# Attention, mixture layer and gated layer on one core: forms of y and the gate-times-value product move from GpSimd to VectorE, and the scheduler gets new urgencies and costs

## The chip, the cores and the metric

The kernel runs on one core of a Trainium2 chip. TensorE (PE) multiplies matrices, VectorE (DVE), ScalarE (ACT) and GpSimd (POOL) work elementwise, SyncE (SP) issues the transfers (DMA). The metric is the device time of one execution in microseconds; a kernel's time is the median of its runs.

## The reference

```
a   = softmax(causal(q @ k.T / 8)) @ v                 # 4 batches, 8 heads, 576 tokens, 64 wide
mem = (phi(q) @ M_prev) / (phi(q) @ z_prev + 1e-6)     # phi(x) = elu(x) + 1
x   = g * mem + (1 - g) * a                            # g = sigmoid(beta); x is 2304 x 512
r   = relu(x @ w_in)                                   # 512 -> 2048
x2  = (s * r * r + b) @ w_out                          # 2048 -> 512
out = (sigmoid(x2 @ w_gate) * (x2 @ w_val)) @ w_out2   # 512 -> 1536 -> 512
```

All of it is float32.

## The kernel before

**Arithmetic.** Each float32 operand of a large product is split into a high part, rounded by ACT, and a low part, the rest, subtracted by DVE (for some of them by POOL). TensorE adds three products of parts.

**Attention (the first third).** There are 16 jobs: job j is one batch and one pair of heads. Jobs 0 to 3, batch 0, take a path of their own (called direct, lines 1000 to 1380). For each job PE transposes k and q (`kt`, `qt`), ACT and DVE split them into `KT` and `QT`, PE makes scores (`sc`, L1139 and L1163 on the direct path, L712 and L738 on the other), DVE masks them and takes the largest of each row into the tile `P` (L692), ACT takes the exponential (`P`, L1179 or L754), PE transposes `P` (`pt`, L1232 or L843, in groups A to D), ACT and DVE copy or split these into `PT_A`, `PT_B`, and PE multiplies them with v (`o`, L1272, or `acc`, L896 on). PE also multiplies phi(q) with the memory (`ret`, L1084). The direct path's results are scaled by DVE into `X` (L1290) and transposed by PE (`xt`, L1306) into x.

**h.** When all of a batch's x is there, PE computes h = x @ w_in (L330, 1536 matmuls in all). This needs no other work beside it and is spread between the later jobs' attention work. Before its use w_in is loaded (`raw_w_in`) and split (`f_w_in` on ACT at L261, then L264 to L273 on DVE). ACT applies relu and r goes to a scratch tensor in DRAM.

**y.** y is summed over 96 steps: 6 windows of 384 tokens, 16 steps each. A step loads r (`rr`), ACT squares it and rounds it to `gh`, DVE subtracts `gl` (L1525), and PE does 12 matmuls (L1540), the last four with `gl`. `gh` and `gl` have rings of four buffers each. Beside this runs the preparation of the gate and value weights in 12 blocks of `raw_gv` (split), `wm` (sums of blocks, DVE L1654), `wp` (high and low parts, ACT L1669 and DVE L1672), stored to a scratch tensor.

**The gated layer.** Windows are taken in three pairs; a pair's gate and value products use a scheme with 7 products in place of 8. It needs sums and differences of quarters of y, the forms: `yf`, `yg` by subtraction (`less`, L1726) and `yt` by splitting (high by ACT at L1717, low at L1721). A pair has 11 such elementwise operations on 128 x 768 elements, of which five are POOL's and six DVE's. Then for 12 groups a pair, six of gate and six of value, PE makes seven products `m` (L1808, 6 matmuls each); DVE adds them up in `set` (L1820), ACT applies the sigmoid, POOL multiplies gate and value into `p` (L1830, 72 operations of 128 x 384 in all), ACT and DVE split `p` into `ps` (L1882, L1895) and PE multiplies with w_out2 (`o`, L1905). The split of w_out2 runs beside the first pair.

**What sets the order.** Nothing of the order is written out by hand. A planner, the class `Plan`, gets each piece of work with its engine, its estimated duration, an urgency and its inputs; it plays the program through with these durations, always starts the ready task with the lowest urgency, and the instructions are emitted in the order found. `late` is how long after its end a task's result reaches another engine. The urgencies come from the table `TUNE`. On the chip every engine takes its own instructions in the order emitted and waits where an input isn't there.

Of the kernel before, what the change touches and what calls it, by code (L numbers as in the profile page):

```python
# [43 lines left out]
class Plan:  # L44
# [6 lines left out]
    def add(self, eng, ns, fn, urgency, reads=(), writes=(), new=(), late=60, size=0, port=0):  # L51

# [104 lines left out]
def attention_moe_kernel(  # L157
# [18 lines left out]
    P = 128  # L176
# [201 lines left out]
    def keys(t):  # L378
        return min((t + 1) * P, S)
# [109 lines left out]
    def mm(n):  # L489
        return max(57, 5 + 0.4375 * n)  # L490
# [4 lines left out]
    def act(n):  # L495
        return 150 + 0.86 * n

    def act2(n):
        return 190 + 0.85 * n

    def dve(n):
        return 152 + 1.05 * n

    def dve2(n):
        return 150 + 1.05 * n
# [43 lines left out]
    def plan_prep(j):  # L549
# [91 lines left out]
        def f_hi():  # L641
# [13 lines left out]
        add("DVE", 1200, phi_s, w, reads=[("phit", j), ("gates", 0)], new=[("nrm", ("nrm", j))])  # L655
# [5 lines left out]
            "ACT", 2 * act(n), f_hi, w, reads=[("ft", j)],  # L661
# [3 lines left out]
            "DVE", 2 * dve(n), lambda: stack_lo(T.pop(("ft", j)), T["FS", j]), w,  # L665
# [32 lines left out]
    def plan_scores(j):  # L698
# [79 lines left out]
        for m, ts in enumerate(groups):  # L778
            w = u + m * AT["tile"]
            if ts[0] < NT4:  # L780
                add(
                    "PE", sum(3 * mm(keys(t)) for t in ts) + 60, lambda ts=ts: score(ts), w,
# [11 lines left out]
            for part in range(2):  # L794
                for t in ts:
                    if part and t == NT4:
# [4 lines left out]
                        "DVE", dve(n) + 90, fn, w + part, reads=[("sc", j, part, ts[0]), ("sums", j)],  # L801
# [4 lines left out]
                        "ACT", 290 + 0.85 * n + 190, lambda e=part, t=t: exps(e, t), w + part,  # L806
                        writes=[("P", j, part, t), sums[part][-1]], reads=[("sums", j)],
                    )
        for part in range(2):
# [3 lines left out]
                "DVE", 450, lambda part=part, cols=cols: rsums(part, cols), w + part,  # L813
# [22 lines left out]
    def plan_products(j):  # L836
# [94 lines left out]
        for m, g in enumerate(gs):  # L931
# [3 lines left out]
            if g not in ("B1", "B2", "D0", "D1"):  # L935
                new.append((tag, ("PT", j, g)))
            key = ("PT", j, "B0" if tag == "PTB" else g)
# [1113 lines left out]
```

## Time and profile before

| | us |
|---|---|
| median of 3 runs | 1063.08 |
| lowest, highest | 1060.46, 1063.38 |
| profiled execution, its time | 1061.53 |
| its span on the chip | 1059.7 |
| PE busy | 1039.0 |
| DVE busy | 693.0 |
| ACT busy | 565.6 |
| POOL busy | 316.9 |

The span runs from the first to the last instruction on the core. The mean granted clock of TensorE was 0.994 of full speed. An engine counts as busy only while it executes: waiting for a semaphore is not in it.

### The profile page before, as it was taken

How to read it: one execution, taken by the hardware profiler on the slowest of the kernel's cores; microseconds unless marked ns; L12 is line 12 of the kernel's file. 1: busy time of each engine (PE TensorE's matmuls, PEld its weight loads, DVE VectorE, ACT ScalarE, POOL GpSimd, SP SyncE). 2: the span in 40 equal slices, each digit the busy share in tenths (PEclk: the TensorE clock that was granted, in tenths of full speed). 3: DMA queues.
4: the chain of work that ended last, by engine and by line, in shares of the span. 5: the costliest groups of instructions: out<-in, count | busy, mean ns of one | idle time of the engine just before them, and what ended most of it. 6: DMA issues, size and time to landing. Idle time of an engine off the chain costs nothing.

```text
span 1059.7 us, 18856 instructions
## 1 busy us (share of the span) xinstructions
PE 1039.0 (98%) x6696; PEld 980.9 (93%) x6696; DVE 693.0 (65%) x1414; ACT 565.6 (53%) x1223; POOL 316.9 (30%) x373
## 2 busy tenths in 40 slices
PE   6999999999999999999999999999999999999998
PEld 4888999999999999999999999998899998899986
DVE  5788887766676637669888765778525576155531
ACT  6587877777777647566867663335212243111230
POOL 2346565544444402310400002445102252033200
PEclk9899999999999999999999999999999999999999
DMA  5544443333222138659699977992368730677400
GB/s 135 132 110 121 132 133 114 102 86 89 77 71 67 51 128 306 212 175 356 220 306 362 381 269 268 325 320 88 116 218 253 254 103 30 206 249 257 153 25 35
DMA packets 159694, 186.46 MB, mean 176 GB/s; under 512 B 70256, under 2 KB 135280, under 8 KB 159600
## 3 DMA queue, kind: packets, MB, share of 16 engines
q1 hardware_dynamic: 158384, 184.96, 53.8%
q8 instruction: 53, 0.87, 0.3%
q10 hardware_dynamic: 1216, 0.30, 0.1%
q14 instruction: 41, 0.34, 0.1%
HBM read 138.03 MB, written 47.19 MB: 175 GB/s over the span
## 4 chain that ended last, share of the span: by engine, by line
PE 94%; ACT 2%; DMA 1%; DVE 1%; issue 1%; SPq 0%; POOL 0%; POOLq 0%; DVEq 0%
PE m L1808 25%; PE h L330 19%; PE y L1540 18%; PE o L1905 14%; PE sc L712 3%; PE acc L896 2%; PE o L1272 2%; PE acc L897 2%; PE pt_B L843 1%; PE acc L900 1%; PE sc L738 1%; PE kt L459 1%; PE pt_A L843 1%; PE pt_D L843 1%; DMA raw_w_in<-in_moe_w_in_dram 1%; PE qt L459 1%
## 5 line engine op out<-in xcount | busy, mean ns | idle before, releaser
L1808 PE MATMUL m<-yt,ws 128*128 128x384 f32 x1512 | 262.8, 334 | 0.0
L1808 PEld LDWEIGHTS m<-yt,ws 128*128 128x128 f32 x1512 | 262.2, 188 | 0.3
L330 PE MATMUL h<-x,w_in 128*128 128x256 f32 (+1 forms) x1536 | 223.9, 300 | 1.0 <-ACT r L340 1.0
L330 PEld LDWEIGHTS h<-x,w_in 128*128 128x128 f32 x1536 | 209.2, 190 | 3.7 <-ACT r L340 1.9
L1820 DVE TENSOR_TENSOR set<-m,set 128x384 f32<-128x384 f32 x252 | 135.7, 555 | 99.3 <-PE m L1808 91.4
L1905 PE MATMUL o<-w_out,ps 128*128 128x512 f32 x648 | 152.1, 396 | 0.6 <-DVE ps L1895 0.6
L1540 PE MATMUL y<-gh,w_out 128*128 128x384 f32 (+1 forms) x768 | 150.8, 338 | 0.7 <-ACT r L340 0.5
L1905 PEld LDWEIGHTS o<-w_out,ps 128*128 128x128 f32 x648 | 121.7, 188 | 29.9 <-DVE ps L1895 1.0
L1540 PEld LDWEIGHTS y<-gh,w_out 128*128 128x128 f32 x768 | 135.4, 188 | 1.4 <-ACT r L340 0.8
L1830 POOL TENSOR_TENSOR p<-set,set 128x384 f32<-128x384 f32 x72 | 75.8, 1057 | 187.7 <-DVE set L1820 187.0
L282 POOL TENSOR_TENSOR w_out<-raw_w_out,w_out 128x512 fp32r<-128x512 f32 x28 | 37.6, 1342 | 215.9 <-DVE set L1820 127.8
L340 ACT ACTIVATE r<-h 128x320 f32<-128x320 f32 (+1 forms) x128 | 51.8, 411 | 67.1 <-PE h L330 59.6
L692 DVE CUSTOM_DVE_ANT_0 P<-sc,mask 128x256 f32<-128x256 f32 (+4 forms) x144 | 68.7, 517 | 23.7 <-PE sc L712 17.4
L1540 PE MATMUL y<-gl,w_out 128*128 128x384 f32 x384 | 82.9, 337 | 0.0
L1816 ACT COPY set<-m 128x384 f32<-128x384 f32 x36 | 17.3, 480 | 111.1 <-PE m L1808 111.1
L770 POOL TENSOR_SCALAR P<-P,rs 128x384 f32<-128x384 f32 (+4 forms) x108 | 65.7, 630 | 25.8 <-DVE rs L766 25.0
L1525 DVE TENSOR_TENSOR gl<-rr,gh 128x384 fp32r<-128x384 f32 x96 | 58.0, 613 | 22.1 <-PE y L1540 15.6
L1895 DVE TENSOR_TENSOR ps<-p,ps 128x512 fp32r<-128x512 f32 x54 | 46.2, 883 | 35.7 <-ACT ps L1882 35.5
L1540 PEld LDWEIGHTS y<-gl,w_out 128*128 128x128 f32 x384 | 68.6, 188 | 0.0
L1824 ACT ACTIVATE set<-set 128x384 f32<-128x384 f32 x72 | 37.6, 524 | 57.1 <-DVE set L1820 57.1
L754 ACT ACTIVATE P<-P,nm 128x384 f32<-128x384 f32 (+4 forms) x108 | 62.5, 581 | 9.4 <-DVE nm L692 9.0
L1882 ACT CAST ps<-p 128x512 fp32r<-128x512 f32 x54 | 32.0, 620 | 65.8 <-PE o L1905 51.8
(185 smaller groups left out, 1504.2 us busy)
## 6 DMA issues: line engine op xcount, KB each, us to landing
ws<-weight_scratch SPq DMA_DIRECT2D x108, 512.0 KB, 4.6
rr<-relu_scratch SPq DMA_DIRECT2D x96, 192.0 KB, 5.6
weight_scratch<-wp SPq DMA_DIRECT2D x36, 512.0 KB, 6.6
raw_w_out<-in_moe_w_out_dram SPq DMA_DIRECT2D x28, 512.0 KB, 6.0
relu_scratch<-r SPq DMA_DIRECT2D x32, 320.0 KB, 2.7
ws<-weight_scratch SPq DMA_DIRECT2D x36, 256.0 KB, 3.1
raw_w_in<-in_moe_w_in_dram SPq DMA_DIRECT2D x16, 512.0 KB, 4.2
relu_scratch<-r SPq DMA_DIRECT2D x32, 256.0 KB, 2.3
```

Of the source, the lines that this page charges most:

```text
L330: nc.tensor.matmul(t[:, :n], wt[:, wi, c], x[:, xi, c], start=(m == 0), stop=(m == 3 * NK - 1))
L340: nc.scalar.activation(rts[b, c0, f - f % 2][:, f % 2, :n], t[:, :n], AF.Relu)
L692: nc.vector.tensor_tensor_reduce(out=pr, in0=ps, in1=mk, scale=1.0, scalar=3e38, op0=ALU.add, op1=ALU.min, accum_out=nm,)
L754: nc.scalar.activation(pr, pr, AF.Exp, bias=T.pop(("nm", j, e, t)), scale=-1.0, accum_out=T["sums", j][:, col : col + 1],)
L770: nc.gpsimd.tensor_scalar(out=pr, in0=pr, scalar1=T["rs", j, part][:, n : n + 1], scalar2=1.0, op0=ALU.mult, op1=ALU.mult,)
L1525: nc.vector.tensor_tensor(out=gl, in0=r_sb.pop(step)[:, :n], in1=gs[step][0][:, :n].bitcast(F32), op=ALU.subtract,)
L1540: nc.tensor.matmul(accs[wi][d][:, : y.shape[1]], w_out_sb[f][:, x, d], y, start=(f == 0 and x == 0 and y is gh), stop=(f == NF - 1 and y i ...
L1808: nc.tensor.matmul(acc, wt[:, a, k : k + P], yt[:, y, c], start=(m == 0), stop=(m == 3 * K2 - 1),)
L1820: nc.vector.tensor_tensor(out=t[:, o], in0=Z["m", z, x], in1=t[:, i], op=ALU.add)
L1830: engine[TIMES[o]].tensor_tensor(out=p[:, f + HF * OF[o][0], OF[o][1]], in0=Z["set", z][:, o], in1=Z["set", zg][:, o], op=ALU.mult,)
L1895: nc.vector.tensor_tensor(out=part(t, 1, i), in0=src(i), in1=part(t, 0, i).bitcast(F32), op=ALU.subtract,)
L1905: nc.tensor.matmul(Z["zo", z], Z["ps", z, i][:, a, k * P : (k + 1) * P], w_out2_sb[f][:, x].rearrange("p c f -> p (c f)"), start=(i == k = ...
```

## The change

- The two groups of forms named above go to DVE: all 11 operations of a pair are now DVE's, 15 more than before in three pairs.
- `TIMES`, the engine of the four products gate x value of a gate group and its value group, is DVE for all: 72 operations.
- P's transposes by PE are a task that in the planner now waits until the target tile `PT` is free. The wait is one of the planner: on the chip the transposes write PSUM and only the copy out of it touches `PT`; what changes is where the transposes stand in PE's order. A matching `p_copy` allocates the tile for whichever group comes first.
- The planner's durations of ACT and DVE work are lower, its `late` for both is higher, and those of PE's score tasks rise by 200 ns.
- All urgencies of `TUNE` are new numbers.

PE's and ACT's instructions are the same ones in another order; DVE has 87 more instructions and POOL 87 fewer.

```diff
 TUNE = {
-    "mem": -190592.6, "lq": 1410.0, "lk": -51988.3, "lv": 48155.5, "lm": 1334.3,
+    "mem": -167048.5, "lq": 2645.2, "lk": -2618.3, "lv": 75766.9, "lm": 2921.8, "q": -48985.8,
...
-    def add(self, eng, ns, fn, urgency, reads=(), writes=(), new=(), late=60, size=0, port=0):
+    def add(self, eng, ns, fn, urgency, reads=(), writes=(), new=(), late=None, size=0, port=0):
+        if late is None:
+            late = {"ACT": 160, "DVE": 145}.get(eng, 60)
...
     def act(n):
-        return 150 + 0.86 * n
+        return 50 + 0.86 * n
...
     def dve(n):
-        return 152 + 1.05 * n
+        return 68 + 1.05 * n
...
-                    "PE", sum(3 * mm(keys(t)) for t in ts) + 60, lambda ts=ts: score(ts), w,
+                    "PE", sum(3 * mm(keys(t)) for t in ts) + 260, lambda ts=ts: score(ts), w,
...
+                if g in ("A0", "B0"):
+                    add("BAR", 0, lambda: None, w, new=[(f"PT{g[0]}", ("PT", j, g))], late=0)
                 add(
                     "PE", flip(nb), lambda g=g: trans(g), w,
-                    reads=sorted({("P", j, e, t) for e, t, k0 in UNITS[g]}),
-                    new=[("s" if nb <= 4 else "w", ("pt", j, g))]
-                    + ([(f"PT{g[0]}", ("PT", j, g))] if g in ("A0", "B0") else []), late=250,
+                    reads=sorted({("P", j, e, t) for e, t, k0 in UNITS[g]}) + [("PT", j, WINS[win][0])],
+                    new=[("s" if nb <= 4 else "w", ("pt", j, g))],
+                    late=250,
                 )
...
-        add("ACT", 675, scaled, u, reads=[("raw", key)], new=[(fl, ("f", key))])
-        add("DVE", **port(1120), fn=rest, urgency=u, writes=[("raw", key)])
+        add("ACT", 573, scaled, u, reads=[("raw", key)], new=[(fl, ("f", key))])
+        add("DVE", **port(950), fn=rest, urgency=u, writes=[("raw", key)])
...
-        plan_split(B21, "B21", "POOL")
+        plan_split(B21, "B21", "DVE")
         plan_split(B22, "B22", "DVE")
-        plan_less("B11", "B12", "B11", "POOL")
+        plan_less("B11", "B12", "B11", "DVE")
         plan_split(T1, "B11", "DVE")
-        plan_less("B12", "B22", "B12", "POOL")
+        plan_less("B12", "B22", "B12", "DVE")
         plan_less("B22", "B22", "B11", "DVE")
-        plan_split(T2, "B22", "POOL")
+        plan_split(T2, "B22", "DVE")
         plan_split(T3, "B12", "DVE")
-        plan_less("B21", "B21", "B22", "POOL")
+        plan_less("B21", "B21", "B22", "DVE")
...
-    TIMES = ("POOL", "POOL", "POOL", "POOL")
+    TIMES = ("DVE", "DVE", "DVE", "DVE")
```

Three places in the new order matter below. In the listings a row is a line, an operation, output and inputs, and the shape.

PE early in the program, behind job 0's first scores; before:

```order
L1084 MATMUL ret_1_206<-mem_144,phi_169 128x65
L1090 MATMUL ret_0_205<-mem_144,phi_169 64x65 x2
L1163 MATMUL sc_4_237<-KT_147,QT_160 128x288 x6
L1232 MATMUL pt_A_262<-ident,P_0_0_230 128x128
L1232 MATMUL pt_A_262<-ident,P_0_1_244 128x128 x2
L1232 MATMUL pt_A_279<-ident,P_1_0_250 128x128
L1232 MATMUL pt_A_279<-ident,P_1_1_258 128x128 x2
L1139 MATMUL sc_0_2_291<-KT_147,QT_160 128x384
```

The same place of the changed kernel:

```order
L1143 MATMUL sc_1_2_205<-KT_151,QT_161 128x384
L1167 MATMUL sc_4_217<-KT_151,QT_161 128x288 x6
L1143 MATMUL sc_0_3_252<-KT_151,QT_161 128x512
L1143 MATMUL sc_1_3_253<-KT_151,QT_161 128x512
L1143 MATMUL sc_0_3_252<-KT_151,QT_161 128x512
L1143 MATMUL sc_1_3_253<-KT_151,QT_161 128x512
L1143 MATMUL sc_0_3_252<-KT_151,QT_161 128x512
L1143 MATMUL sc_1_3_253<-KT_151,QT_161 128x512
L1236 MATMUL pt_A_277<-ident,P_0_0_228 128x128
L1236 MATMUL pt_A_277<-ident,P_0_1_233 128x128 x2
```

All scores of job 0 now stand ahead of the transposes of its first `P` and of `ret`, which stood between them. In the same way all of job 1's scores now stand ahead of job 0's first `o`; SP loads the first `raw_w_in` and job 1's q ahead of `mem`, which they followed; ACT has the first `f_w_in` ahead of job 0's first exponential, and it stood behind the copy of `PT_A`.

DVE in the y stage at the first steps of the third window (`gl_2` on), where the forms of the first pair become possible; before:

```order
L1525 TENSOR_TENSOR gl_1_7175<-rr_1_7005,gh_1_7152 128x384
L1525 TENSOR_TENSOR gl_2_7181<-rr_2_7031,gh_2_7173 128x384
L1584 TENSOR_SCALAR yf_7179<-y_1_6761,sb_s,sb_c 128x384
L1584 TENSOR_SCALAR yf_7179<-y_3_6763,sb_s,sb_c 128x384
L1525 TENSOR_TENSOR gl_3_7207<-rr_3_7042,gh_3_7203 128x384
L1721 TENSOR_TENSOR yt_0_7205<-yf_6757,yt_0_7205 128x768
L1525 TENSOR_TENSOR gl_4_7232<-rr_4_7081,gh_4_7228 128x384
```

and of the changed kernel, from behind `gl_1` of that window:

```order
L1677 TENSOR_TENSOR wp_1_7156<-wm_7110,wp_1_7156 128x512
L1677 TENSOR_TENSOR wp_2_7162<-wm_7110,wp_2_7162 128x512
L1677 TENSOR_TENSOR wp_3_7167<-raw_gv_1_6922,wp_3_7167 128x256
L265 TENSOR_SCALAR raw_gv_0_7016<-raw_gv_0_7016 128x512
L268 SCALAR_TENSOR_TENSOR raw_gv_0_7016<-raw_gv_0_7016 128x512
L1589 TENSOR_SCALAR yf_7190<-y_1_6765,sb_s,sb_c 128x384
L1589 TENSOR_SCALAR yf_7190<-y_3_6767,sb_s,sb_c 128x384
L274 SCALAR_TENSOR_TENSOR raw_gv_0_7016<-f_gv_0_7170,raw_gv_0_7016 128x512
L1726 TENSOR_TENSOR yt_0_7214<-yf_6780,yt_0_7214 128x768
L1726 TENSOR_TENSOR yt_1_7216<-yf_6780,yt_1_7216 128x768
L1731 TENSOR_TENSOR yf_6780<-yf_7190,yf_6780 128x768
L1726 TENSOR_TENSOR yt_6_7219<-yf_7190,yt_6_7219 128x768
```

Before, the window's second and third `gl` stand next to each other; now twelve operations, weight blocks and forms, stand between them.

DVE at the end of the first pair's products, ahead of the first `ps` that follow the last group; before:

```order
L1820 TENSOR_TENSOR set_11_9649<-m_11_4_9696,set_11_9649 128x384
L1721 TENSOR_TENSOR yt_5_9704<-yf_8360,yt_5_9704 128x768
L1820 TENSOR_TENSOR set_11_9649<-m_11_6_9708,set_11_9649 128x384
L1721 TENSOR_TENSOR yt_6_9731<-yf_8732,yt_6_9731 128x768
L1895 TENSOR_TENSOR ps_0_2_9736<-p_8898,ps_0_2_9736 128x512
```

and of the changed kernel:

```order
L1825 TENSOR_TENSOR set_11_9645<-m_11_4_9697,set_11_9645 128x384
L1835 TENSOR_TENSOR p_8927<-set_11_9645,set_5_9554 128x384 x3
L1825 TENSOR_TENSOR set_11_9645<-m_11_6_9709,set_11_9645 128x384
L1835 TENSOR_TENSOR p_8927<-set_11_9645,set_5_9554 128x384
L1900 TENSOR_TENSOR ps_0_2_9736<-p_8927,ps_0_2_9736 128x512
```

The forms of the next pair that stood there have moved away, and the four products `p` of the last group stand in DVE's row instead of POOL's.

## Rows read from the trace of the kernel before

**Rows 1.** The page's span in 40 equal slices of 26.5 us, tenths.

```profile
PE   6999999999999999999999999999999999999998
...
PEclk9899999999999999999999999999999999999999
```

**Rows 2.** The page's chain of work that ended last, by engine.

```profile
PE 94%; ACT 2%; DMA 1%; DVE 1%; issue 1%; SPq 0%; POOL 0%; POOLq 0%; DVEq 0%
```

**Rows 3.** Busy time in stretches of the span; columns in the first row.

```profile
core 0: us, PE busy (x) PEld busy (x) DVE busy (x) ACT busy (x) POOL busy (x), PEclk, DMA share, GB/s
0.00:20.00 20.00, 12.02 (x81) 9.52 (x82) 9.30 (x34) 9.81 (x20) 6.08 (x34) 0.91 0.65 152
20.00:40.00 20.00, 17.60 (x138) 15.79 (x137) 13.95 (x38) 12.48 (x25) 4.01 (x4) 0.83 0.55 125
...
620.00:642.00 22.00, 22.00 (x127) 22.00 (x127) 8.48 (x18) 9.74 (x21) 0.00 (x0) 1.00 0.90 314
642.00:722.00 80.00, 80.00 (x463) 80.00 (x462) 60.23 (x112) 31.75 (x60) 34.60 (x31) 1.00 0.84 300
```

**Rows 4.** The chain between 25 and 97 us: start, us, what (parts of it).

```profile
28.41 2.79 PE o L1272 x12
...
33.42 1.29 PE o L1272 x12
...
94.33 0.66 DVE KT L584
...
96.36 2.56 PE h L330 x12
```

**Rows 5.** Timeline of DVE, 27 to 34 us: start, us, ..., [idle before <-releaser].

```profile
27.97 0.23 DVE L1103 SCALAR_TENSOR_TENSOR rm<-ret,gtu 128x5 f32<-128x5 f32 x2 [0.79 <-PE ret L1090]
...
31.24 0.16 DVE L1285 SCALAR_TENSOR_TENSOR ro<-o,iomu 128x4 f32<-128x4 f32 x1 [1.93 <-PE o L1272]
...
33.64 0.82 DVE L1028 SCALAR_TENSOR_TENSOR QT<-qt,QT 128x640 fp32r<-128x640 f32 x1 [1.56 <-ACT phi L1019]
```

**Rows 6.** Timeline of ACT, 17 us.

```profile
17.40 0.68 ACT L261 ACTIVATE f_w_in<-raw_w_in 128x512 f32<-128x512 f32 x1 [0.96 <-DMA raw_w_in<-in_moe_w_in_dram]
```

**Rows 7.** The page's costliest groups: sums, gate x value, largest of rows, `gl`.

```profile
L1820 DVE TENSOR_TENSOR set<-m,set 128x384 f32<-128x384 f32 x252 | 135.7, 555 | 99.3 <-PE m L1808 91.4
...
L1830 POOL TENSOR_TENSOR p<-set,set 128x384 f32<-128x384 f32 x72 | 75.8, 1057 | 187.7 <-DVE set L1820 187.0
...
L692 DVE CUSTOM_DVE_ANT_0 P<-sc,mask 128x256 f32<-128x256 f32 (+4 forms) x144 | 68.7, 517 | 23.7 <-PE sc L712 17.4
...
L1525 DVE TENSOR_TENSOR gl<-rr,gh 128x384 fp32r<-128x384 f32 x96 | 58.0, 613 | 22.1 <-PE y L1540 15.6
```

**Rows 8.** Tile `yf`: duration ns min/median/max, first and last start us, forms.

```profile
L1721 DVE TENSOR_TENSOR yt<-yf,yt x10: 946/952/2611, 509.3 to 751.7; 128x768 fp32r<-128x768 f32 x10
...
L1726 POOL TENSOR_TENSOR yf<-yf,yf x4: 1847/1984/2179, 511.9 to 744.8; 128x768 f32<-128x768 f32 x4
```

**Rows 9.** Timeline of DVE, 512 to 517 us.

```profile
512.27 2.61 DVE L1721 TENSOR_TENSOR yt<-yf,yt 128x768 fp32r<-128x768 f32 x1
514.81 2.34 DVE L1672 TENSOR_TENSOR wp<-wm,wp 128x512 fp32r<-128x512 f32 x1
```

**Rows 10.** Timeline of POOL, 512 us.

```profile
511.89 2.18 POOL L1726 TENSOR_TENSOR yf<-yf,yf 128x768 f32<-128x768 f32 x1
```

**Rows 11.** Busy time between 469 and 568 us, columns as in Rows 3.

```profile
469.00:568.00 99.00, 98.47 (x565) 98.21 (x564) 86.42 (x155) 70.67 (x141) 10.70 (x5) 1.00 0.82 287
```

**Rows 12.** DVE's waits there: us in total, times, longest.

```profile
DVE gl L1525 <- PE y L1540: 5.8, 11, 1.2
DVE gl L1525 <- ACT gh L1520: 3.0, 4, 0.9
```

**Rows 13.** Timeline of PE at 736 us.

```profile
735.72 1.43 PE L1905 MATMUL o<-w_out,ps 128*128 128x512 f32 x5 [0.58 <-DVE ps L1895]
```

**Rows 14.** Timeline of DVE at 734 us.

```profile
734.16 6.03 DVE L1895 TENSOR_TENSOR ps<-p,ps 128x512 fp32r<-128x512 f32 x3
```

More of the change, by code (lines that the diff above doesn't have):

```diff
@@ L654, in plan_prep @@
         )
-        add("DVE", 1200, phi_s, w, reads=[("phit", j), ("gates", 0)], new=[("nrm", ("nrm", j))])
+        add("DVE", 950, phi_s, w, reads=[("phit", j), ("gates", 0)], new=[("nrm", ("nrm", j))])
         add("POOL", **port(1260), fn=phi_n, urgency=w, reads=[("nrm", j)], writes=[("phi", j)])
@@ L800, in plan_scores @@
                     add(
-                        "DVE", dve(n) + 90, fn, w + part, reads=[("sc", j, part, ts[0]), ("sums", j)],
+                        "DVE", dve(n) + 10, fn, w + part, reads=[("sc", j, part, ts[0]), ("sums", j)],
                         writes=[("P", j, part, t)],
@@ L805, in plan_scores @@
                     add(
-                        "ACT", 290 + 0.85 * n + 190, lambda e=part, t=t: exps(e, t), w + part,
+                        "ACT", 278 + 0.85 * n, lambda e=part, t=t: exps(e, t), w + part,
                         writes=[("P", j, part, t), sums[part][-1]], reads=[("sums", j)],
@@ L812, in plan_scores @@
             add(
-                "DVE", 450, lambda part=part, cols=cols: rsums(part, cols), w + part,
+                "DVE", 300, lambda part=part, cols=cols: rsums(part, cols), w + part,
                 reads=sums[part] + [("sums", j), ("gates", 0)], new=[(f"rs{part}", ("rs", j, part))],
@@ L934, in plan_products @@
             tag = "PT" + ("B" if g[0] in "BD" else g[0])
-            if g not in ("B1", "B2", "D0", "D1"):
+            if tag != "PTB":
                 new.append((tag, ("PT", j, g)))
+            elif g == "B0":
+                add("BAR", 0, lambda: None, w, new=[(tag, ("PT", j, g))], late=0)
             key = ("PT", j, "B0" if tag == "PTB" else g)
@@ L1121, in prep_direct @@
         add(
-            "DVE", 1450, mem_norm, w, reads=[("ret", j, 0), ("ret", j, 1), ("gates", 0)], writes=[("MX", j)],
+            "DVE", 1000, mem_norm, w, reads=[("ret", j, 0), ("ret", j, 1), ("gates", 0)], writes=[("MX", j)],
         )
@@ L1185, in scores_direct @@
                 add(
-                    "PE", sum(3 * mm(keys(t)) for t in ts) + 60, lambda ts=ts: score(ts), w,
+                    "PE", sum(3 * mm(keys(t)) for t in ts) + 260, lambda ts=ts: score(ts), w,
                     reads=[("QT", j), ("KT", j)],
@@ L1203, in scores_direct @@
                     add(
-                        "DVE", dve(n) + 90, fn, w + part, reads=[("sc", j, part, ts[0])],
+                        "DVE", dve(n) + 10, fn, w + part, reads=[("sc", j, part, ts[0])],
                         writes=[("P", j, part, t)],
@@ L1207, in scores_direct @@
                     add(
-                        "ACT", 290 + 0.85 * n, lambda e=part, t=t: exps(e, t), w + part,
+                        "ACT", 185 + 0.85 * n, lambda e=part, t=t: exps(e, t), w + part,
                         writes=[("P", j, part, t)],
@@ L1685, in plan_blocks @@
             add(
-                "DVE", **port(850), fn=lambda part=part: sums(part), urgency=u,
+                "DVE", **port(675), fn=lambda part=part: sums(part), urgency=u,
                 reads=[k0, k1, "bar2"], writes=[("wm", n)] if part else [],
@@ L1733, in plan_split @@
         def plan_split(i, name, eng):
-            add("ACT", 840, lambda: hi(i, name), u, reads=base + [key(name)] + fresh, new=[(f"t{i}", ("yt", pi, i))])
+            add("ACT", 735, lambda: hi(i, name), u, reads=base + [key(name)] + fresh, new=[(f"t{i}", ("yt", pi, i))])
             add(
-                eng, **port(950 if eng == "DVE" else 1850), fn=lambda: lo(i, name, eng), urgency=u,
+                eng, **port(870 if eng == "DVE" else 1850), fn=lambda: lo(i, name, eng), urgency=u,
                 reads=base + [key(name)], writes=[("yt", pi, i)],
@@ L1741, in plan_less @@
             add(
-                eng, **port(950 if eng == "DVE" else 1850), fn=lambda: less(o, x, y, eng), urgency=u,
+                eng, **port(870 if eng == "DVE" else 1850), fn=lambda: less(o, x, y, eng), urgency=u,
                 reads=base + [key(z) for z in (x, y) if z != o], writes=[key(o)],
```

28 lines of the change are left out of this document (14 added, 14 removed), and 12 rows, old and new, of the table TUNE.

## The prediction

> **What bounds the kernel now.** I read the slices of the span first, then the chain, then the stretches. TensorE is full from about 100 us to the end: in the slices PE shows 9 tenths everywhere but in the first (6) and the last (8) [rows 1], and the chain is PE for 94% [rows 2]. In the stretches of the gated layer PE is busy for 80.00 of 80.00 us [rows 3]. So an engine other than PE can give nothing there: POOL's gate x value has 187.7 us of idle ahead of it, waiting for DVE's sums [rows 7], and nobody waits for POOL. Time can be won only where PE waits: in the first 100 us, where PE is busy 12.02 of 20 and 17.60 of 20 us at a granted clock of 0.91 and 0.83 [rows 3], and in one hole at 735 us [rows 13]. Busy time overstates PE's work in the head, for at that clock the same 12 matmuls take 2.79 us that take 1.29 us a little later [rows 4]. What PE waits for there is the chain of direct-path work through ACT and DVE; it ends with ACT's and DVE's split for `KT` at 94.33 us, and PE's run of h that begins at 96.36 us [rows 4] is the start of the full stretch.
>
> **The change part by part.**
>
> *The head: a gain of 6 us, between 2 and 9.* Two things follow from the orders. First, seven largest-of-row instructions of job 4 no longer stand ahead of the direct path's last `X` on DVE, and one weight operation does. At the mean of 0.517 us [rows 7] seven are 3.6 us; one weight operation is about 0.7; started back to back they overlap a little, so I count 2.3 us less work for DVE ahead of the last `X`, on which the whole of batch 0's h waits. That is the lower end, since it holds if DVE's idle time stays as it is. Second, all scores of jobs 0 and 1 come earlier on PE, so DVE has largest-of-row work where it now stands idle: between 27 and 34 us it waits 0.79 us for `ret`, 1.93 us for `o` and 1.56 us for ACT [rows 5], together 4.28 us. With job 1's maxima there instead, that wait goes. 2.3 and 4.28 are 6.6; I take 6, since some of the maxima that fill the gap are only moved ahead of `X` of job 0, whose transposes then come later. The upper end adds what ACT loses: ACT stands 0.96 us for the first `raw_w_in` and then spends 0.68 us on it [rows 6], ahead of job 0's last exponentials and job 1's `QT`. In the changed order SP issues that load ahead of `mem`, and ACT does the operation in a gap it has before the first exponential: 1.64 us, and something for a granted clock that PE, better fed, may get back sooner; 6.6 + 1.6 + some 1 us is 9. What is late next: `ret` of job 0, since `mem` is now behind q and k of the next jobs on SP's queue, and `vals`, which the `o` at 28.41 us needs. The changed PE order puts `ret` behind most of job 0's transposes, which is the cover for the first, and all of job 1's scores ahead of `o`, which is the cover for the second. If that cover is too thin, rival C holds.
>
> *Attention after 100 us: nothing, plus or minus 2 us.* PE is at 9 tenths in each slice and stays so as long as h is there to fill; the changed order leaves more of h for later. The waits for P's transposes are waits of the planner, so they cost no semaphore, only another place in the order.
>
> *Forms to DVE and the y stage: a loss of 1.5 us, between 0 and 5.* From 469 to 568 us DVE is busy 86.42 of 99.00 us [rows 11]. PE goes at 2.08 us a step: 22.00 us for 127 matmuls [rows 3] times the 12 of a step. With a ring of four, DVE's `gl` can lead PE by at most four steps, less the last four matmuls of a step (0.69 us) and the 0.61 us of `gl` itself [rows 7]: 7.0 us. That DVE reaches this limit is seen in its waiting for PE 11 times ahead of `gl` [rows 12]. In the changed order more weight blocks and the forms stand ahead of the fifth window: counted at start-to-start paces, which for each shape are a little below its duration (0.87 us for a form against 0.952 [rows 8]), DVE has 96.6 us of work in a stretch that takes PE 99.0. So it keeps up on average, and the question is the dense spot behind the third window's second `gl`: twelve operations, 8.0 us at that pace, against 7.0 of lead and 2.08 of a step. There is no stall at that pace with a full lead. I added up the lead step by step along the new order: it is 0.5 us of stall at these paces, 1.6 us if all are 5% longer, 4.2 if 10%. I take 1.5 and keep 0 and 5.
>
> POOL's forms took 1.98 us where DVE's take 0.95 [rows 8], and they slowed DVE beside them: DVE's `yt` at 512.27 us took 2.61 us and the `wp` behind it 2.34 us [rows 9], while POOL had its form from 511.89 us on [rows 10]; a `yt` is usually 0.95 us [rows 8]. So of the price of the forms on DVE a part comes back, 1.7 us on this one instruction. This is why I stay nearer to 0 than to 5.
>
> The Trainium skill, "SBUF — State Buffer", section "SBUF: two separate sides", says that VectorE with two SBUF inputs and GpSimd take turns on one shared port pair, by an exclusive lock. The trace agrees at the one place above; by the rule alone each form taken off POOL would give DVE back up to its 2 us, and the y stage would lose nothing, 1.5 us less than my sum.
>
> *Gate x value on DVE: nothing.* 72 operations at about the 0.555 us of a `set` [rows 7] are 40 us more of DVE work, four for each gate group and its value group, whose 84 matmuls take 84 x 80.00/463 = 14.5 us [rows 3]. From 642 to 722 us DVE is busy 60.23 of 80.00 us [rows 3]; this stretch holds 5.5 such pairs of groups, so `p` adds 5.5 x 2.2 = 12 us and makes 72 to 73 of 80. DVE keeps up, with the banks of `m` as a buffer. If it did not, the excess would be PE's to the full; I give this 0 and carry the risk into rival B. POOL's 75.8 us become free, which nobody waits for.
>
> *The hole at 735 us: a gain of 0.9 us.* PE waited 0.58 us for `ps` [rows 13] while DVE's three `ps` took 6.03 us in all [rows 14] where three of the usual length leave no hole. In the changed order no form stands on POOL and none stands right ahead of these `ps`. PE lost the 0.58 and, by the same wait, some of the matmuls just ahead of it; I take 0.9, between 0.6 and 1.2.
>
> *The sum.* 1061.53 us of the profiled execution - 6 - 0.9 + 1.5 = 1056.1 us. The median of the runs shown is 1063.08, 1.55 us above that execution; on its basis the forecast is 1057.7 us.
>
> **The rivals.** *B, slower: DVE becomes the bound in the y stage.* DVE's idle time from 469 to 568 us is 99.00 - 86.42 = 12.6 us [rows 11], of which 3.0 are waits for ACT ahead of `gl` [rows 12], not only for PE. If these stay where they are, because `gl` still waits for `gh`, the 96.6 us of work need 96.6 + 12.6 = 109.2 us, against 99.0 + 7.0 of lead: 3.2 us of stall. If in addition the work goes by full durations, in the proportion in which 86.42 stands to the same work counted at paces (76.2), it is 109.7 + 12.6 = 122.3, 16.3 us of stall. The middle is 9.8 us, for 1066 us, and the far end gives 1072.5; I price it at 1069. It decides from the point where DVE's work between two `gl` exceeds 2.08 us a step for longer than the 7.0 us lead. For it speaks the dense spot and that ACT already makes `gl` wait; against it, that most of the idle time is waiting for PE, which a busier DVE does not have. Chance 0.16.
>
> The Trainium skill, "Perfetto Trace Analysis", section "Optimizing Scalar/DVE Operations", speaks for this rival: where DVE is saturated it would move work to ScalarE or GpSimd, the reverse of this change, though it adds that between these two it might not help. No row shows DVE saturated over 40 us or more.
>
> *C, no change: the head's gain does not come.* The chain of the head is then one of transfers and ACT, and DVE's filled gaps open again elsewhere: `ret` waits for `mem`, loaded nine queue entries later, `o` for `vals`, three entries later. Then only 0.9 us is won and 1.5 lost, within 0.3%; with a quarter of the head's gain left it is 1062.5. Against it, PE has transposes and scores to do in that time. Chance 0.22.
>
> *D: the move of gate x value and forms alone decides nothing.* Were the reordering inert, PE stays full and the time is 1063; this is part of C.
>
> **How the numbers follow.** Forecast 0.62 with its own range from 1051 (head 9, y stage 0, attention -2) to 1062 (head 2, y stage 3); C 0.22 at 1060 to 1065; B 0.16 at 1066 to 1072.5. The range 1051 to 1066 leaves out the upper half of B and a little below. A measurement tells a difference of about 0.3% here, 3.2 us: faster is below 1059.9, slower above 1066.3. The forecast lies below 1059.9 for nearly all its weight, C is nearly all within, B for most above: faster 0.61, same 0.24, slower 0.15.
>
> **What would show it.** In the changed profile: PE's full stretch beginning at about 90 us, not 96; DVE's idle time ahead of job 0's `X` gone; nothing on PE waiting for `gl` by more than some 1.5 us in all; `p` on DVE at about 0.55 us with PE busy 80 of 80 us beside it; no hole at the end of the first pair. It is wrong if PE's waits for `mem`, `vals` or `kt` in the first 40 us grow by as much as DVE's shrink, or if the waits for `gl` between 500 and 570 us come to 5 us or more.

## The result

The changed kernel is slower: its median is 1068.22 us over 13 executions (1065.06 to 1075.43), against 1062.56 us over 13 of the kernel before; the ratio is 1.0055, with a 95% interval from 1.0032 to 1.0077. The profiled execution took 1065.06 us with a span of 1063.3 us, 3.6 us more than the span before; it is the fastest of its 13, and 4.6 us above the fastest of the kernel before.

PE is still 98% of the span. Its chain is another one, though [rows 2]: the page of the changed kernel gives the chain that ended last as

```profile
PE 85%; DVE 5%; DMA 4%; ACT 2%; issue 2%; SPq 1%; POOL 1%; ACTq 0%; DVEq 0%; POOLq 0%
```

It was PE for 94%; now DVE and DMA have a place in it. One row splits the change in two. Behind the last h, PE waits 0.53 us for ACT and then begins y's second window: by then all of attention, all of h and the first window are done in either kernel. The timelines of PE have it in the kernel before at

```profile
472.85 1.32 PE L1540 MATMUL y<-gh,w_out 128*128 128x384 f32 x6 [0.53 <-ACT r L340]
```

and in the changed kernel at

```profile
472.47 1.68 PE L1545 MATMUL y<-gh,w_out 128*128 128x384 f32 x8 [0.53 <-ACT r L341]
```

So attention and h together are only 0.4 us shorter, and the later part, from there to the end of the span, is 1063.3 - 472.47 = 590.8 us against 1059.7 - 472.85 = 586.9: 4.0 us longer.

**The later part.** PE's waits between 476 and 645 us in the changed kernel (us in total, times, longest):

```profile
PE y L1545 <- ACT gh L1525: 2.0, 2, 1.1
PE y L1545 <- DVE gl L1530: 0.8, 1, 0.8
```

The page's groups of weight loads show the same waits from the side of the loads (busy, mean ns | idle before, releaser):

```profile
L1545 PEld LDWEIGHTS y<-gh,w_out 128*128 128x128 f32 x768 | 135.2, 188 | 3.7 <-ACT gh L1525 2.8
...
L1545 PEld LDWEIGHTS y<-gl,w_out 128*128 128x128 f32 x384 | 68.3, 188 | 1.5 <-DVE gl L1530 1.3
```

The same two groups of the kernel before had

```profile
L1540 PEld LDWEIGHTS y<-gh,w_out 128*128 128x128 f32 x768 | 135.4, 188 | 1.4 <-ACT r L340 0.8
...
L1540 PEld LDWEIGHTS y<-gl,w_out 128*128 128x128 f32 x384 | 68.6, 188 | 0.0
```

3.7 + 1.5 - 1.4 = 3.8 us of new idle time, nearly the whole 4.0. (For the matmuls themselves the waits add up to 2.8 us; the eight matmuls behind a wait for `gh` also take 1.66 to 1.68 us, where eight take 1.56 us at 491.52 us.)

There are three places. At 511.68 us PE waits 1.06 us for `gh`; the timeline of ACT ahead of it:

```profile
503.17 0.52 ACT L1525 CAST gh<-rr 128x384 fp32r<-128x384 f32 x1
...
505.93 1.24 ACT L1594 ACTIVATE yf<-y,sb_c,sb_s 128x384 f32<-128x384 f32 x2 [0.30 <-PE y L1545]
507.06 2.48 ACT L1722 CAST yt<-yf 128x768 fp32r<-128x768 f32 x3
509.44 0.66 ACT L1674 CAST wp<-raw_gv 128x512 fp32r<-128x512 f32 x1
510.01 0.66 ACT L262 ACTIVATE f_gv<-raw_gv 128x512 f32<-128x512 f32 x1
...
511.12 0.51 ACT L1525 CAST gh<-rr 128x384 fp32r<-128x384 f32 x1
```

From one `gh` to the next 7.95 us pass, where PE wants one each 2.08 us: in between stand weight blocks, the evictions of y and three casts of forms. At 525.70 us PE waits 0.90 us for `gh`; there ACT itself waits:

```profile
518.95 0.83 ACT L1722 CAST yt<-yf 128x768 fp32r<-128x768 f32 x1
524.01 0.69 ACT L262 ACTIVATE f_gv<-raw_gv 128x512 f32<-128x512 f32 x1 [4.23 <-DVE raw_gv L274]
...
525.14 0.51 ACT L1525 CAST gh<-rr 128x384 fp32r<-128x384 f32 x1
```

For 4.23 us a weight block's `f_gv` stands at the head of ACT's queue and the `gh` that PE needs stands behind it. What it waits for is at the end of this stretch of DVE's timeline:

```profile
519.29 0.95 DVE L1726 TENSOR_TENSOR yt<-yf,yt 128x768 fp32r<-128x768 f32 x1
520.16 0.55 DVE L1530 TENSOR_TENSOR gl<-rr,gh 128x384 fp32r<-128x384 f32 x1
520.63 0.95 DVE L1726 TENSOR_TENSOR yt<-yf,yt 128x768 fp32r<-128x768 f32 x1
521.50 0.68 DVE L1677 TENSOR_TENSOR wp<-raw_gv,wp 128x512 fp32r<-128x512 f32 x1
522.10 0.42 DVE L265 TENSOR_SCALAR raw_gv<-raw_gv 128x512 int32<-128x512 int32 x1
522.55 0.69 DVE L268 SCALAR_TENSOR_TENSOR raw_gv<-raw_gv 128x512 int32<-128x512 int32 x1
523.28 0.69 DVE L274 SCALAR_TENSOR_TENSOR raw_gv<-f_gv,raw_gv 128x512 int32<-128x512 int32 x1
```

DVE works through forms and weight blocks without a gap and is late with the block. The third place is a `gl` at 589 us, 0.8 us.

**Attention.** In busy time (columns as in [rows 3]) the kernel before and then the changed one:

```profile
0.00:100.00 100.00, 85.16 (x725) 73.41 (x726) 74.66 (x209) 68.07 (x138) 38.24 (x73) 0.93 0.50 123
100.00:472.00 372.00, 370.99 (x2853) 355.29 (x2851) 257.76 (x589) 264.30 (x640) 155.24 (x202) 1.00 0.41 126
```

```profile
0.00:100.00 100.00, 87.83 (x754) 76.20 (x755) 78.04 (x213) 69.78 (x146) 40.49 (x75) 0.97 0.54 131
100.00:472.00 372.00, 368.98 (x2825) 351.80 (x2823) 250.23 (x586) 259.39 (x635) 152.61 (x201) 1.00 0.40 123
```

In the first 100 us PE is busy 2.7 us more, at a higher granted clock. The last 128 x 128 transpose `xt` of batch 0 starts at 88.2 us, where it was 93.7 us (tile `xt`, L1310, min/median/max and first and last start):

```profile
L1310 PE MATMUL xt<-ident,X x16: 272/273/332, 39.4 to 88.2; 128*128 128x128 f32 x16
```

But from 100 to 472 us PE is idle 372.00 - 368.98 = 3.0 us, against 1.0 before.

The earlier `xt` is not 5.5 us of PE's time. The h of batch 0 comes in two pieces of tokens, and in the kernel before the first piece's matmuls ran ahead of the last `xt`. The text ahead of the prediction says that h waits for all of a batch's x; it doesn't. Before:

```profile
76.42 1.67 PE L330 MATMUL h<-x,w_in 128*128 128x256 f32 x12
85.76 1.67 PE L330 MATMUL h<-x,w_in 128*128 128x256 f32 x12
93.55 0.44 PE L1306 MATMUL xt<-ident,X 128*128 128x128 f32 x2 [0.20 <-POOL X L1298]
```

In the changed kernel no h stands ahead of it:

```profile
88.04 0.44 PE L1310 MATMUL xt<-ident,X 128*128 128x128 f32 x2
88.67 1.71 PE L331 MATMUL h<-x,w_in 128*128 128x256 f32 x12
```

3.3 of the 5.5 us are these 24 matmuls, which now come later. Up to this `xt` PE was busy 79.48 of 93.55 us and is now busy 75.87 of 88.04: 14.1 us idle before, 12.2 now, 1.9 less. The 2.0 us more of idle time after 100 us take that back.

One execution's clock does not explain it. In the kernels below with attention as before the last `xt` starts at 93.7 to 97.7 us, and with the new attention (e12, e15 and e16 apart) at 88.2 to 92.5, and 99.1 in one; y's second window begins at 472.85 to 475.34 us and at 472.13 to 475.38, and 482.21 in that one.

**The hole at the end of the first pair** [rows 13, 14] is still there:

```profile
735.35 3.21 PE L1910 MATMUL o<-w_out,ps 128*128 128x512 f32 x13
739.08 2.13 PE L1910 MATMUL o<-w_out,ps 128*128 128x512 f32 x8 [0.52 <-DVE ps L1900]
```

### The profile page after: what moved, and what is told of

Read it like the earlier page. It is cut to its first block, busy times and chain, and to the rows that moved or that the text cites. A ratio compares the mean times of both kernels' runs of the same rounds, so it can differ in the third digit from the quotient of the medians.

```text
span 1063.3 us, 18771 instructions
## 1 busy us (share of the span) xinstructions
PE 1040.5 (98%) x6696; PEld 979.8 (92%) x6696; DVE 712.7 (67%) x1501; ACT 561.9 (53%) x1223; POOL 209.6 (20%) x286
## 4 chain that ended last, share of the span: by engine, by line
PE 85%; DVE 5%; DMA 4%; ACT 2%; issue 2%; SPq 1%; POOL 1%; ACTq 0%; DVEq 0%; POOLq 0%
PE m L1813 25%; PE h L331 18%; PE o L1910 14%; PE y L1545 14%; PE sc L713 3%; PE acc L897 2%; PE acc L898 2%; DMA raw_gv<-in_moe_w_gate_dram 1%; DMA raw_w_in<-in_moe_w_in_dram 1%; PE pt_B L844 1%; PE o L1276 1%; PE sc L739 1%; PE acc L901 1%; DMA weight_scratch<-wp 1%; PE pt_D L844 1%
## 5 line engine op out<-in xcount | busy, mean ns | idle before, releaser
L1530 DVE TENSOR_TENSOR gl<-rr,gh 128x384 fp32r<-128x384 f32 x96 | 55.2, 585 | 52.3 <-PE y L1545 36.6
L1900 DVE TENSOR_TENSOR ps<-p,ps 128x512 fp32r<-128x512 f32 x54 | 35.7, 688 | 38.4 <-ACT ps L1887 38.2
L1525 ACT CAST gh<-rr 128x384 fp32r<-128x384 f32 (+1 forms) x96 | 49.3, 514 | 17.7 <-issue 9.7
```

The lines of the kernel that those rows point to most:

```text
L1525: nc.scalar.copy(gh, r_sb[step])
L1530: nc.vector.tensor_tensor(out=gl, in0=r_sb.pop(step)[:, :n], in1=gs[step][0][:, :n].bitcast(F32), op=ALU.subtract,)
```

## The experiments

The first question is which part of the program and which part of the change lose the time. The later part's length, read as above from one row and the span, and PE's idle time in 476 to 640 us (164.00 us less PE's busy time) stand in the table; the ratio is that of the executions' times to those of the kernel before, run beside each. In e14, e15 and e16 the second window begins after 476 us, so 0.53 us of their idle time is the wait ahead of it: y itself has 1.70, 0.00 and 0.00 us.

| kernel | attention | from y on: urgencies / durations | engine | y's second window at | to the end | PE idle 476:640 | ratio [95%] |
|---|---|---|---|---|---|---|---|
| before | old | old / old | POOL | 472.85 | 586.9 | 0.13 | |
| changed | new | new / new | DVE | 472.47 | 590.8 | 2.75 | 1.0055 [1.0032, 1.0077] |
| e1 | old | new / new | DVE | 475.34 | 590.3 | 2.53 | 1.0046 [1.0021, 1.0072] |
| e2 | new | old / old | POOL | 472.38 | 586.9 | 0.13 | 0.9992 [0.9971, 1.0012] |
| e3 | old | old / old | DVE | 474.75 | 586.8 | 0.00 | 1.0001 [0.9981, 1.0021] |
| e4 | new | new / new | POOL | 472.13 | 606.2 | 7.00 | 1.0173 [1.0155, 1.0191] |
| e5 | new | old / new | DVE | 475.03 | 591.7 | 3.11 | 1.0050 [1.0026, 1.0075] |
| e6 | new | old / old, `late` old | DVE | 473.49 | 588.0 | 0.67 | 0.9987 [0.9960, 1.0014] |
| e7 | new | new / new, `late` old | DVE | 472.25 | 594.7 | 3.41 | 1.0052 [1.0030, 1.0073] |
| e8 | new | old / old | DVE | 475.38 | 585.6 | 0.00 | 0.9979 [0.9957, 1.0000] |
| e9 | new | new / old | DVE | 475.02 | 589.5 | 0.18 | 1.0036 [1.0014, 1.0059] |
| e10 | new | new / ACT's old | DVE | 473.44 | 593.6 | 4.21 | 1.0078 [1.0051, 1.0104] |
| e11 | new | new / DVE's old | DVE | 474.08 | 587.1 | 0.40 | 0.9997 [0.9977, 1.0018] |
| e12 | new, durations old | new / old | DVE | 510.71 | 592.7 | 1.59 | 1.0393 [1.0363, 1.0423] |
| e13 | new | new / DVE's weight blocks old | DVE | 473.79 | 589.3 | 2.17 | 1.0014 [0.9989, 1.0040] |
| e14 | new | new / DVE's others old | DVE | 482.21 | 590.6 | 2.23 | 1.0019 [0.9993, 1.0045] |
| e15 | new, `lm` 2400 | as e8 | DVE | 480.17 | 585.6 | 0.53 | 1.0048 [1.0036, 1.0061] |
| e16 | new, `lm` 1334.3 | as e8 | DVE | 502.91 | 585.7 | 0.53 | 1.0153 [1.0127, 1.0179] |

**e1 and e2: attention against the rest.** Durations and `late` are given to the planner by part of the program: a flag is raised before the first task of y's part.

```diff
+LATER = []
...
     def dve(n):
-        return 152 + 1.05 * n
+        return (68 + 1.05 * n) if LATER else 152 + 1.05 * n
...
+    LATER.append(1)
     for f in range(NF):
         plan_w_out(f)
```

So in e1 attention's instructions stand in the order of the kernel before, and from the second window on the order is that of the changed kernel; e2 is the reverse.

> Attention and h in the order of the kernel before (its urgencies, costs and transposes for that part), everything from y on as in the changed kernel. In the changed kernel's trace PE loses 3.3 us more than before between 500 and 640 us, in waits for ACT's gh (2.0) and DVE's gl (0.8). Theory Y (the loss is the y stage's): 3.3 us above before, ratio about 1.003. Theory H (attention's order costs, in runs with a lower granted clock more than in the profiled one): within 0.1% of before.

> The reverse: attention and h in the order of the changed kernel, everything from y on as before, POOL's forms and products included. Theory Y: within 0.1% of before, since what the head gains by 100 us (3.7 us less lost on PE) is given back by 472 us. Theory H: 2 to 5 us above before, ratio 1.002 to 1.005, with a lower mean granted clock in most runs.

The loss came with the later part: e1 is as slow as the changed kernel, with waits of PE at the same two operands in 476 to 645 us:

```profile
PE y L1537 <- ACT gh L1517: 1.8, 2, 0.9
PE y L1537 <- DVE gl L1522: 0.8, 1, 0.8
```

e2 can't be told from the kernel before. Theory Y holds.

**e3 and e4: the engine against the order.**

```diff
-    TIMES = ("POOL", "POOL", "POOL", "POOL")
+    TIMES = ("DVE", "DVE", "DVE", "DVE")
...
-        plan_split(B21, "B21", "POOL")
+        plan_split(B21, "B21", "DVE")
...
```

> The kernel before with only the engine of forms and of gate x value changed to DVE; urgencies and costs are the old ones, so attention stands word for word as before. If DVE's extra load is the cause of the y stage's loss whatever the order: 3 us or more above before. If the new urgencies are the cause: within 1 us of before, or 1 us faster, since the hole at 735 us and the slowed operations beside POOL go.

> The changed kernel with forms and gate x value back on POOL, all urgencies and costs new. If the move is the cause of the y stage's loss: 3 us below the changed kernel, about 1065 us. If the new order is: as the changed kernel or up to 3 us slower, for POOL's forms slow DVE beside them in the dense place.

e3 makes this edit (all five forms) in the kernel before: no difference that can be told (the interval is 0.2% to either side), and PE has no idle time at all from 476 to 640 us. 87 operations more on DVE cost nothing, and POOL's lost work gives nothing. e4 undoes it in the changed kernel: 18 us slower than before. Neither expectation for e4 held, the first in direction and the second in size. In its order POOL's slower operations are in the way twice, in y and ahead of the first `o` (PE's waits from 476 to 760 us):

```profile
PE y L1545 <- ACT gh L1525: 7.0, 3, 2.7
PE o L1910 <- ACT ps L1887: 6.4, 1, 6.4
```

In both the planner has made the order from y on anew for the other engine. So with the new urgencies and durations DVE is needed as the engine, and with the old ones it makes no difference. The move by itself doesn't lose the time; the order that the planner makes from the new numbers does.

**e5 to e8: urgencies, durations or `late`.**

```diff
 TUNE = {
-    "wos": 638.2, "gv": 498.7, "gvs": 2228.3, "y": 1125.9, "lead": -638.3, "lr": -823.2,
+    "wos": 214.5, "gv": 1724.7, "gvs": 1424.3, "y": 426.2, "lead": -946.0, "lr": -1293.6,
```

This (in the layout of the change, and with all urgencies from y on) is e5. e7 sets `late` back:

```diff
-            late = {"ACT": 160, "DVE": 145}.get(eng, 60)
+            late = 60 if LATER else {"ACT": 160, "DVE": 145}.get(eng, 60)
```

> The changed kernel with the old urgencies from y on; attention's urgencies, all the new durations and `late`, and DVE as the engine stay. Its DVE order still has runs of 10 and 12 operations between two gl (the changed kernel: 12 and 11). Theory U (the new urgencies of the y stage cost): as the kernel before, about 1062 us. Theory D (the planner's shorter durations make it bunch work between two gl): as the changed kernel, 4 to 6 us above before, with PE waiting for gh or gl at the runs.

> The reverse: new urgencies everywhere and DVE as the engine, but from y on the old durations and the old `late`. At most 6 operations stand between two gl of the third window. Theory U: as the changed kernel. Theory D: 1061 us, as the kernel with the changed attention and the old later part, and no wait of PE over 0.3 us between 475 and 640 us.

> The changed kernel with only `late` (the time from a result to another engine) back at 60 ns from y on; the shorter durations stay. If the durations make the loss: 3 us or more above before, with runs of 9 and 12 operations still between two gl. If the longer `late` makes it: about 1062 us.

> The changed kernel with only the durations back at the old values from y on; the longer `late` stays. If the durations make the loss: 1061 to 1062 us. If `late` does: 3 us or more above before.

e6 and e8 carry the old urgencies from y on as well, unlike their texts: the table has them as they ran. They are read against e5, then. e5 to e8 differs in the planner's durations alone, and PE's idle time goes from 3.11 to 0.00 us and the later part from 591.7 to 585.6 us; e5 to e6 in durations and `late`: 3.11 to 0.67, which is one wait, above the 0.3 us that was expected. e5 says that the urgencies aren't the cause of the waits in y, e7 that `late` isn't. Theory D holds with the old urgencies; whether it does with the new ones was left to e9.

**e9 to e11: whose durations.** The old durations from y on in the changed kernel, for both engines (e9), for ACT's work (e10) and for DVE's (e11):

```diff
     def act2(n):
-        return 90 + 0.84 * n
+        return (190 + 0.85 * n) if LATER else 90 + 0.84 * n
...
     def dve2(n):
-        return 67 + 1.05 * n
+        return (150 + 1.05 * n) if LATER else 67 + 1.05 * n
...
-        add("DVE", **port(950), fn=rest, urgency=u, writes=[("raw", key)])
+        add("DVE", **port(1120 if LATER else 950), fn=rest, urgency=u, writes=[("raw", key)])
```

> The changed kernel, its urgencies and `late` everywhere, with only the durations of ACT's and DVE's work from y on at their old values. (The kernels e6 and e8 carried the old urgencies from y on as well, other than their texts say; this one is what the text of e8 describes.) If the durations alone make the loss: 1061 to 1063 us, with under 2 us of waits on PE between 475 and 750 us. If they only help together with the old urgencies: 1066 us or more.

> As e9, but only ACT's durations are old, DVE's stay new. In the changed kernel's trace a square and the rounding behind it take 0.97 us on ACT (498.03 to 499.00), where the planner counts 0.83; old it counts 1.03. If ACT's understated time makes the loss (PE waits for gh first): 1061 to 1063 us. If DVE's does: 1066 us or more, with PE still waiting for gh or gl in three places.

> As e9, but only DVE's durations are old, ACT's stay new. If ACT's understated time makes the loss: 1066 us or more. If DVE's does (the three operations of a weight split take 1.67 us in the trace, 499.60 to 500.67 and 0.61; the planner counts 1.56, old 1.81; a sum of four wm 1.47 against 1.35, old 1.70): 1061 to 1063 us.

With DVE's old durations the waits in y are gone: 0.40 us idle, the one wait being

```profile
PE y L1548 <- DVE gl L1533: 0.4, 1, 0.4
```

and the time is that of the kernel before. With ACT's alone they grow, to 4.21 us:

```profile
PE y L1548 <- ACT gh L1528: 4.2, 3, 2.5
```

I had thought that ACT's understated pair of square and rounding makes the loss, since PE waits for `gh` first. That fell: `gh` is only the last link. e9 has no waits in y either (0.18 us), as its first theory said, but a larger hole at the first pair's end, for which its median, 1065.97 us, came out above that theory's 1061 to 1063 and at the second one's 1066:

```profile
739.16 0.51 PE L1913 MATMUL o<-w_out,ps 128*128 128x512 f32 x1 [1.62 <-ACT ps L1890]
740.45 1.91 PE L1913 MATMUL o<-w_out,ps 128*128 128x512 f32 x7 [0.78 <-DVE ps L1903]
```

**e12: attention with the old durations.**

> The changed kernel with all durations old, attention's too; urgencies, `late`, the engine and the wait for PT are new. In the changed kernel PE loses 3.5 us less than before up to 120 us and some 2.8 us more from 120 to 472 us. If the new durations make the second part too, PE loses 17 us there as before, not 20, and if the new urgencies make the first, that gain stays: 1059 to 1060 us. If both come from the durations: as e9 or slower by up to 1 us. If the old durations don't go with the new urgencies in attention: 1064 us or more.

The last case holds, far beyond its number: 1104.37 us, with y's second window 38 us later than in the changed kernel. The busy time from 120 to 472 us:

```profile
120.00:472.00 352.00, 331.94 (x2542) 312.60 (x2541) 231.02 (x544) 236.48 (x583) 141.44 (x192) 0.99 0.35 106
```

PE is idle for 20 us of 352, where the changed kernel has 3. Attention's new urgencies hold only with the new durations they stand beside.

**e13 and e14: which of DVE's durations.** e13 takes back those of the weight blocks (rest, joined, sums), e14 all others (gl, wp, forms, set, p, ps).

> The changed kernel with only the planner's durations of the weight blocks on DVE at the old values from y on (rest 1120, joined 690, a half of the sums 850 ns); gl, forms, wp and all else new. In the changed kernel's trace rest takes 0.456 and 0.615 us from start to start, 1.07 in all, against 0.95 in the planner's table; gl takes 0.469 against 0.470 and a form 0.869 against 0.870. If the understated weight blocks make the loss: 1062 to 1064 us, PE losing under 2 us between 475 and 640 us. If the lack of any margin in the other durations does: 1066 us or more.

> The changed kernel with DVE's other durations (gl, wp, yf, forms, set, p, ps) at the old values from y on, the weight blocks' new. If the understated weight blocks make the loss: 1066 us or more. If the lack of any margin in the other durations does: 1062 to 1064 us.

Neither theory holds alone: PE is idle in y for 2.17 us in the one and 1.70 us in the other, where the changed kernel has 2.75 and e11, which takes back both, 0.40. By their times neither can be told from the kernel before. The understated weight block seems to matter no more than the durations that agree with the trace; this fits a lack of margin in all of them better than one wrong number, but no run adds a margin and nothing else.

One rival goes through all of these: any new number makes the planner find another order, so a single kernel may be luck. Against it stands the table. With DVE's new durations from y on (changed, e1, e4, e5, e7, e10) PE is idle in y for 2.5 to 7.0 us; with its old ones (before, e2, e3, e6, e8, e9, e11, e15, e16) for 0.67 us at most, and for 1.59 us in e12, whose attention ends 38 us later.

**e15 and e16: the head.** The changed kernel's PE waits 2.4 us for `mem` ahead of `ret`. Both kernels are e8 with more urgent loads of it:

```diff
-"lm": 2921.8
+"lm": 2400.0
```

> The kernel of e8 (attention's new urgencies, from y on old urgencies and durations, DVE as the engine) with the memory's loads more urgent (2400 in place of 2921.8), so that job 0's mem stands behind the first raw_w_in on SP's queue, ahead of the k and q that it followed. In the changed kernel's order PE waits 2.3 to 2.4 us for that load ahead of ret, and the granted clock then falls, to 0.66 from 20 to 30 us in one execution and to 0.50 to 0.74 from 20 to 60 us in another (e14), which ended 10 us later at the same order. If this wait is what costs the head: no wait for mem on PE and 1058 to 1061 us, ratio to before 0.994 to 0.997. If another wait takes its place: as e8, 1062 us.

> As e15 with 1334.3, the value of the kernel before: mem of jobs 0 and 1 ahead of all but the first loads, the first raw_w_in and q behind them as before the change. If the wait for mem costs the head and the early raw_w_in gives nothing: as e15. If the early raw_w_in and q are what the head gains from: 1062 us or more.

Both are slower than the kernel before. In e15 the wait for `mem` is 1.6 us and, in its place, there are new ones up to 120 us, among them

```profile
PE ret L1083 <- DMA mem<-in_z_prev_dram: 1.6, 1, 1.6
PE pt_A L1231 <- ACT P L1178: 1.5, 1, 1.5
PE o L1271 <- DVE PT_B L1250: 1.3, 1, 1.3
```

and y's second window begins at 480.17 us. e16 has no wait for `mem` left and is slower still. Neither tests the wait alone, for the planner makes the whole order of the head new for such a number, and what that changes weighs more than the wait. What of e16's loss is the late `raw_w_in` and what the other moves stays open, since both changed.

No version beats both kernels clearly. e8, with attention of the changed kernel, DVE as the engine and the old urgencies and durations from y on, has the shortest later part with no wait of PE from 476 us to the end; its ratio of 0.9979 has an interval that ends at 1.0000.

## Why the prediction was wrong

It forecast 1057.7 us, 6 us faster on the profiled execution; the changed kernel is 5.7 us slower in the median and 3.5 us in the profiled execution (1065.06 against 1061.53).

- **What bounds the kernel** was right: PE is full but for its waits, and the time moved only where these did.
- **Gate x value on DVE, nothing:** right. `p` takes 0.557 us (median) on DVE, PE is busy 80.00 of 80.00 us from 640 to 720 us, DVE 65.32 us there where 72 to 73 were reckoned, and e3 has the move by itself at a ratio of 1.0001.
- **The head, a gain of 6 us:** wrong, and the step that failed is the place where the gain was read. The prediction took the last `X` as that on which the whole of batch 0's h waits. The rows above show 24 matmuls of that h ahead of the last `xt` in the kernel before and none in the changed one. So `xt` came 5.5 us earlier, and PE's run of h began at 88.67 us, as the prediction's first sign had it; but 3.3 us of that is h put off, and only 1.9 us less idle time. That 5.5 lies close to 6 is luck: DVE's waits that were to go came back under other names, 2.65 us for `ret` at 21.91 us where `ret` cost 0.79 [rows 5]. The next step, "attention after 100 us: nothing, plus or minus 2 us", then cost the upper end of its range, 2.0 us of idle time, and y's second window begins only 0.4 us earlier. Rival C was right that the head's gain would not come; whether for its reason isn't shown. Its waits exist (`mem` 2.4 us, `vals` 0.2 us), but e15 and e16 don't test them alone.
- **The y stage, a loss of 1.5 us, between 0 and 5:** DVE's dense spots do cost, as the prediction said, but the size was not right: the later part is 4.0 us longer, and e1 shows 3.4 us (590.3 less 586.9) with attention as before. The step that failed is the sum of the lead along DVE's order alone. It let `gl` decide and took `gh` as given, with ACT always ready. In the trace two of three waits are for `gh`, because ACT's queue has casts of forms and pieces of weight blocks bunched as DVE's has, and in one of them `f_gv` stands there for 4.23 us for DVE. The sum at 10% longer work, 4.2 us, lies nearer, though it follows `gl` alone as well; the working had it and took the lower one on the ground that POOL's forms no longer slow DVE. That relief is real and lies off the path: in e3 no `ps` takes over 0.694 us where one took 2.344 us before, and the time is the same.
- **The hole at 735 us, a gain of 0.9 us:** wrong. DVE's `ps` no longer stand at 2 us each, but PE still waits 0.52 us where it waited 0.58 [rows 13]. The last `m`, its `set`, `p`, ACT's `ps` and DVE's `ps` follow one on the other, and 13 matmuls of `o` are all that PE has meanwhile. In e8 the matmuls of `o` run on there without a wait.
- **Rival B** was nearest: DVE bounds y at its dense places through ACT's queue, as its first term said (3.2 us; the later part lost 4.0). That the median of 1068.22 us lies close to its price of 1069 is luck: the price holds the head's gain, which did not come, and a stall of 9.8 us or more. **Rival D**, that the move decides nothing, is shown by e3 for the old urgencies and durations; e4 shows that the new ones can't do without it.
- **The chances:** slower had 0.15. The order was read as it stands at paces from the trace, and so with the planner's own optimism. Two sums in the working are a little off and change nothing of this: a head of 2 us with 3 us lost in y gives 1063.2 us, not 1062, and a quarter of the head's gain 1062.2, not 1062.5.

What stays open: the medians differ by 5.7 us and the two profiled spans by 3.6 us; the interval of the ratio (3.4 to 8.2 us) reaches down to that difference, and no run settles the remainder.

The Trainium skill, "SBUF — State Buffer", section "SBUF: two separate sides", has a VectorE operation with two SBUF inputs and one of GpSimd block each other by a lock. The trace agrees: DVE's `ps` took up to 2.344 us while POOL worked on forms, and at most 0.694 us in e3 and in the changed kernel, where POOL has none. No effect on the time can be told (e3).

## What to carry to other kernels

Given measured start-to-start paces, the list scheduler here packed DVE's queue without slack, and what slipped on the chip became waits of PE, which bounds the kernel; durations with some 80 ns of margin an instruction made the better order in y, though they were the less exact ones. Test a planner's durations and its urgencies apart, and by part of the program: the new durations were needed by attention's new urgencies (e12) and harmful in y (e5, e8). Where a gain is read at one instruction that comes earlier, count what else stood ahead of it: here h had only changed places with attention. Where two engines feed the bounding one, follow both queues: an instruction that waits at the head of the second engine's queue for the first passes the first one's lateness on.

## What the runs showed of the hardware

One order of attention gave 482.21 us at y's second window in e14 and 472.47 us in the changed kernel, though up to 404 us every engine has its instructions in the same order in both. The busy time from 20 to 50 us (columns as in [rows 3]; the third figure from the right is the granted clock), first of the changed kernel:

```profile
20.00:30.00 10.00, 8.66 (x72) 7.27 (x72) 5.66 (x19) 6.06 (x12) 1.30 (x1) 0.66 0.57 135
30.00:40.00 10.00, 8.76 (x74) 7.63 (x72) 9.75 (x24) 7.10 (x13) 2.18 (x2) 1.00 0.83 185
40.00:50.00 10.00, 10.00 (x111) 9.23 (x111) 7.33 (x27) 6.07 (x14) 4.28 (x7) 1.00 0.57 157
```

and of e14:

```profile
20.00:30.00 10.00, 8.37 (x54) 6.86 (x54) 4.58 (x18) 6.26 (x13) 1.29 (x1) 0.56 0.59 138
30.00:40.00 10.00, 10.00 (x54) 8.73 (x54) 7.52 (x19) 5.04 (x9) 0.00 (x0) 0.50 0.64 141
40.00:50.00 10.00, 10.00 (x50) 10.00 (x49) 5.42 (x12) 3.49 (x7) 3.27 (x3) 0.50 0.44 114
```

In both PE waited over 2 us for `mem` at the start of this stretch. In the one the granted clock came back to 1.00 (the upper level, 2.4 GHz) at 30 us; in the other it stayed at 0.50 (1.2 GHz) to beyond 50 us, with PE busy throughout, and 50 to 54 matmuls went through where 74 to 111 did. By the same matmul of the order e14 was 0.3 us behind at 20 us and 10.9 us at 50 us, while PE was idle for less time (1.6 us of these 30 against 2.6). So the 9.7 us come from the clock. The 13 executions of the changed kernel go with it: 1065.06 us at a mean granted clock of 0.997, 1075.43 us at 0.984. In a head of this kind a microsecond should be believed only after several executions.
